# Logits of blocks 0 and 2 spread over other steps, and tile 7's normalisation and transposes moved

## The chip, the cores and the metric

The kernel runs on one core of a Trainium2 chip. The metric is the device time of one execution in microseconds (us), smaller is better. The core's engines run side by side, each through its own list of instructions in order, and wait for one another by semaphores: TensorE (PE, matmuls; PEld is its weight loading), VectorE (DVE), ScalarE (ACT), GpSimd (POOL) and SyncE (SP, which here only issues transfers). Matmuls write into banks of PSUM, and a bank can be written anew only when its readers are done.

## The reference

Three parts follow one another: attention over keys and values that are pooled by 8, a feed-forward network with the activation elu, and a second one that is routed, each token going to one of 8 experts by the largest gate logit. q, k and v are 8 x 8 x 576 x 64 in float32, so there are 4608 tokens of width 512; the first network's inner width is 2048, each expert's 1024.

```python
def _attn_ref(q, k, v) -> np.ndarray:
    ...
    scale = 1.0 / np.sqrt(D)
    k_p = k.reshape(B, H, Sp, pool, D).mean(axis=3)
    v_p = v.reshape(B, H, Sp, pool, D).mean(axis=3)
    scores = scale * np.matmul(q, k_p.transpose(0, 1, 3, 2))
    scores = scores - np.max(scores, axis=-1, keepdims=True)
    attn = np.exp(scores)
    attn = attn / (np.sum(attn, axis=-1, keepdims=True) + 1e-09)
    return np.matmul(attn, v_p).astype(np.float32)

def _moe_ref(x, w_in, w_out) -> np.ndarray:
    h = x @ w_in
    alpha = 1.0
    g = np.where(h > 0.0, h, alpha * (np.exp(np.minimum(h, 0.0)) - 1.0))
    return (g @ w_out).astype(np.float32)

def _moe2_ref(x, w_gate, w1, w2) -> np.ndarray:
    ...
    logits = x @ w_gate
    expert_idx = np.argmax(logits, axis=1)
    ...
    for e in range(E):
        ...
        h = np.maximum(xe @ w1[e], 0.0)
        ye = h @ w2[e]
        out[mask] = gate_w[mask, None] * ye
    return out.astype(np.float32)
```

## The kernel before

The 4608 tokens are 36 tiles of 128, and three tiles make a block, so there are 12 blocks. The stretch in question runs attention and the first network for the blocks, and the gate for each block after it. It is cut into 192 *steps*: a step multiplies one block by one sixteenth of the first network's inner width. Blocks 0 and 1 share steps 0 to 31 in alternating groups (20 to 27 belong to block 1, 28 to 31 to block 0); from step 32 on each block has 16 steps in a row: block 2 has 32 to 47, block 3 has 48 to 63, block 4 has 64 to 79.

In step n, PE computes *h*, 12 matmuls (`g1_mm`, L507), into one of two h banks in turn, then what else is due, and last *y* of step n-2, 9 matmuls (`g2`, L549), which add up in three banks, one for each tile, over the block's steps. ACT and DVE make the elu out of h: ACT runs three activations (`elu_a`, L517 to L519, the last writes th), DVE two instructions (`elu_b`, L524 and L525, called *g* below). The second frees the h bank for step n+2. Then ACT casts g to gh (L531) and DVE takes the rest gl (L532): y is computed as a sum of products of such high and low parts. Weights of the first network are split in the same manner in steps 0 to 27; DVE's part of this are *bits* (L226 to L232) and wol (L246).

Everything else is hung into steps by a table: `at(n, slot, function)` puts a piece of work into a slot of step n, and `step(n)` runs the slots in a fixed order. What matters is the later half of it: `act_mid` stands just behind g, then come y's matmuls, `pe_end`, then `evac` and `y_evac`, which copies y out of its banks when a block's sum is complete, then `dve_mid`, gh and gl, `act_end` and `end`. This order is the order on each engine; nothing reorders it later.

Attention of a tile t takes: scores on PE (`s_mm`, L411, into two banks), maxima on DVE (L418), exponentials on ACT (L427), the normalisation on DVE (`s_norm`, L431 to L433), transposes on PE (`t_mm`, L463, into two banks) with their copies on ACT (`t_copy`, L471), or for tiles from 9 on a turn on DVE (L447) with copies (`q_move`, L455), and the product with the values (`pv_mm`, L480), copied as xh and xl (L493, L494) for the first network. The scores, transposes, pv and the position counts of the gate take their banks from one ring of three.

The gate of a block, placed by `route_at(blk, n0, per)`, computes 24 logits (8 experts by 3 tiles), each one DVE instruction over 128 x 512 elements (`r_logit`, L600), from the token rows yr and a row of gate weights that SP has loaded. `per` lists how many stand in each step from n0 on: the first of a step in `dve_mid`, the others at `end`. In the step after the last of them comes the *top* (`r_top`: maximum, comparison, exponentials), one later the *weights* (`r_weight`, L641 to L653), which complete the token rows and let SP store them by three transfers (L647), and two further on the position count on PE (`r_count`, L663 and L664, one bank) with the *put* on DVE at `end` (`r_put`, L669 to L673) and three table writes on GpSimd. The token rows of a block are one buffer, yr, used by each block in turn; the rows of block 0 were parked and came back in three spare tiles (part).

Of the kernel before, what the change touches and what calls it, by code (L numbers as in the profile page):

```python
# [10 lines left out]
F32 = mybir.dt.float32  # L11
# [8 lines left out]
P = 128  # L20
B, H, S, D = 8, 8, 576, 64
# [5 lines left out]
TB = 3  # L27
# [3 lines left out]
NF = DFF // P  # L31
NE = 8
# [66 lines left out]
def fused_kernel(ctx: ExitStack, tc: tile.TileContext, q, k, v, w_in, w_out, w_gate, w1, w2, cst, out):  # L99
# [38 lines left out]
    mrpool = ctx.enter_context(tc.tile_pool(name="mrpool", bufs=1, side="right"))  # L138
# [357 lines left out]
    ys, yrows, lgs, pes = {}, {}, {}, {}  # L496
# [74 lines left out]
        yr = y_rows(blk, fetched.pop(x) if x is not None else None)  # L571
        yrows[blk] = [yr[:, j] for j in range(TB)]

    fetched = {}

    def y_park(blk, x, plus=None):
        yr = y_rows(blk, fetched.pop(plus) if plus is not None else None)
# [2 lines left out]
    def y_fetch(x, j):  # L580
        t = spool.tile([P, S], F32, tag="st", name=f"part{x}_{j}")
        nc.sync.dma_start(t[:, :DM], yparts[x][j * P:(j + 1) * P, :])
        fetched.setdefault(x, []).append(t[:, :DM])
        if x == 2:
            yrows.setdefault(0, []).append(t[:, :ROW])

    def y_join():
        for j in range(TB):
            nc.vector.tensor_add(yrows[0][j][:, :DM], yrows[0][j][:, :DM], ys[0][j])
# [5 lines left out]

    def r_logit(blk, e, j):
        if (e, j) == (0, 0):
            lgs[blk] = mrpool.tile([P, TB, NE], F32, tag="lg", name=f"lg{blk}")
        junk = mrpool.tile([P, DM], BF16, tag="junk", name=f"junk{blk}_{e}_{j}")
        nc.vector.scalar_tensor_tensor(  # L600
            junk, yrows[blk][j][:, :DM], 1.0, pes[blk, e], op0=ALU.mult, op1=ALU.mult, accum_out=lgs[blk][:, j, e:e + 1]
        )

    def r_logits(blk, e):
        for j in range(TB):
            r_logit(blk, e, j)
# [84 lines left out]
    LAG = 2  # L691
# [3 lines left out]
    def at(n, slot, fn, *args):  # L695
        events.setdefault((n, slot), []).append((fn, args))
# [3 lines left out]
    def score_at(t, n):  # L700
        at(n, "pe_end" if t == 7 else "pe_mid", s_mm, t)
        for hh in range(2):
            at(n, "dve_mid" if t == 7 else "dve_pre", s_max, t, hh)
        at(n, "act_end" if t in (6, 7) else "act_mid", s_exp, t, 0)
        n += t not in (7, 8)
        at(n, "act_end" if t in (7, 8) else "act_mid", s_exp, t, 1)
        at(n, "dve_mid" if t == 6 else "end", s_norm, t)

    def turn_at(t, n):
        at(n + 1, "end", q_turn, t)  # L710
# [3 lines left out]
    def trans_at(t, n):  # L714
        at(n, "pe_end" if t in OUT else "pe_mid", t_mm, t)
        for hh in range(2):
            at(n, "act_end" if t in OUT else "act_mid", t_copy, t, hh, nc.scalar.copy)
        out = OUT.get(t, ((n, "pe_end"), (n + 1, "pre")))
        at(*out[0], pv_mm, t)
        at(*out[1], pv_copy, t)  # L720
# [1 line left out]
    at(2 * NF - 2, "end", s_wide)  # L722
    first_of = {b: b * S // P for b in range(B)}
    SCORE = {6: (20, "pe_mid"), 7: (24, "pe_mid"), 8: (28, "pe_mid")}
    TRANS = {6: 23, 7: 26, 8: 30}
    OUT = {
        6: ((28, "pe_end"), (29, "pre")),
        7: ((29, "pe_end"), (30, "pre")),
# [2 lines left out]
    for t in range(2 * TB, NT):  # L731
        if t not in SCORE:
            blk, j = divmod(t, TB)
            SCORE[t] = (NF * (blk - 1) + 5 * j - 2 if blk > 3 else 2 * NF - 1 + 5 * j, "pe_mid")
            if t > T_TURN:
                at(SCORE[t][0], "pe_mid", pv_mm, t - 1)
                at(SCORE[t][0], "act_mid", pv_copy, t - 1)
            at(SCORE[t][0] - 6, "end", a_load, t)
        else:
            at(SCORE[t][0] - 6, "end", a_load, t)  # L740
        score_at(t, SCORE[t][0])
        if t >= T_TURN:
            turn_at(t, SCORE[t][0] + (t == T_TURN))
        else:
            trans_at(t, TRANS[t])
    at(NF * (NBLK - 1) - 2, "pe_mid", pv_mm, NT - 1)
# [42 lines left out]
    for x, (w, c) in enumerate(chunks):  # L789
        n = 2 + x  # L790
# [11 lines left out]
    for j in range(TB):  # L802
        at(4 * QF + 1 + j + (j == 2), "end", y_fetch, 0, j)
        at(6 * QF + 2 + j, "end", y_fetch, 1, j)
        at(7 * QF + 1 + j, "act_end", y_fetch, 2, j)

    def route_at(blk, n0, per):
        at(n0 - 3, "end", r_gate_load, blk, 0)
        at(n0 - 2, "end", r_gate_load, blk, 1)
        at(n0 - 1, "end", r_gate_load, blk, 2)  # L810
        n = 0
        for x in range(NE * TB):
            e, j = divmod(x, TB)
            at(n0 + n, ("dve_mid", "end", "end", "end")[x - sum(per[:n])], r_logit, blk, e, j)
            if j == TB - 1 and e + 3 < NE:
                at(n0 + n, "end", r_gate_load, blk, e + 3)
            if x + 1 == sum(per[:n + 1]):
                n += 1
        n += n0
        at(n, "dve_mid", r_top, blk)  # L820
        at(n + 1, "dve_mid", r_weight, blk)
        if blk < last - 1:
            at(n + 3, "pe_mid", r_count, blk)
            at(n + 3, "end", r_put, blk)

    route_at(1, 30, [2, 3, 3, 1, 1, 2, 3, 3, 3, 3])
    route_at(0, 41, [2] + [3] * 6 + [2, 2])
    route_at(2, 3 * NF + LAG + 1, [2, 2, 2, 2, 3, 3, 3, 3, 4])
    for blk in range(3, last):
        route_at(blk, NF * (blk + 1) + LAG, [3, 2, 3, 2, 3, 2, 3, 2, 2, 2])  # L830

# [663 lines left out]
    for k in range(1, len(main)):  # L1495
        kind, prev = main[k][0], main[k - 1][0]
        for u in range(TILES[kind]):
            if kind == "T":
                n = 4 * k - 2
            elif prev == "T":  # L1500
                n = 4 * k - TILES[kind] + u
            else:
                n = 4 * k - 1
            (trans_late if prev != "T" and u > 1 else trans_at).setdefault(n, []).append((main[k], u))
    moves, casts_first = {}, set()
    for k in range(TURN_FROM, len(main)):
        it, far = main[k], main[k - 1][0] == "T"
        if it[0] != "T":
# [3 lines left out]
            n = 4 * k - 4 if far else 4 * k - 1  # L1512
# [21 lines left out]
    def logits(n):  # L1534
        for x in range(6 * n, 6 * n + 6):
            e, j = divmod(x, TB)
            r_logit(last, e, j)
            if j == TB - 1 and e + 3 < NE:
                r_gate_load(last, e + 3)
# [166 lines left out]
```

## Time and profile before

| | |
|---|---|
| median of 3 runs | 1350.76 us (1349.97 to 1350.95) |
| the profiled execution | 1353.46 us, its span 1351.7 us |
| PE busy | 1333.7 us, 99% of the span |
| DVE busy | 1034.3 us, 77% |
| ACT busy | 813.0 us, 60% |
| GpSimd busy | 206.0 us, 15% |
| chain that ended last | PE 81%, DVE 7%, issue 5%, ACT 3%, DMA 3% |

The profile is of one execution. A row of a timeline gives the start and the length of an instruction (or of some alike in a row, "x4") and in brackets how long the engine had idled before it, and which instruction released it. Matmuls are pipelined, so that the lengths of neighbours overlap: distances from start to start are to be used. The chain that ended last is followed back from the last instruction, at each step to what released it.

### The profile page before, as it was taken

To read this page: it belongs to the slowest core of one execution; us is meant where nothing else is said; L and a number is where in the kernel's file an instruction comes from. 1 tells how busy PE (TensorE), PEld (TensorE's weight loads), DVE (VectorE), ACT (ScalarE), POOL (GpSimd) and SP (SyncE) were. 2 spreads that over 40 slices of the span, in tenths; PEclk is the share of its full clock that TensorE was granted. 3 is DMA by queue.
4 is the path that set the end of the run, shared out by engine and by line. 5 is a ranking of instruction groups with operands and counts; after the bars stand their busy time and mean duration, and the time that the engine had idled before them with its cause. 6 is when DMAs were issued, how large, how long until landed. Compare 5 with 4: busy or idle time off the path is not lost.

```text
span 1351.7 us, 23691 instructions
## 1 busy us (share of the span) xinstructions
PE 1333.7 (99%) x8365; PEld 1149.8 (85%) x8366; DVE 1034.3 (77%) x2463; ACT 813.0 (60%) x1977; POOL 206.0 (15%) x208
## 2 busy tenths in 40 slices
PE   8999999999999999999999999999999999999998
PEld 5799888888888889888888888988887888778787
DVE  7899888998887879797978787885768666646371
ACT  6777766676767676676666665562455444535261
POOL 0011011101111211111210000020313142112020
PEclk9999999999999999999999999999999999999999
DMA  9257443657464574545571432466577357758470
GB/s 344 76 175 211 124 100 82 87 77 71 72 86 74 69 85 56 93 65 81 70 98 48 64 36 52 79 167 122 180 132 157 124 180 265 261 198 309 148 272 24
DMA packets 109146, 169.43 MB, mean 125 GB/s; under 512 B 15510, under 2 KB 53016, under 8 KB 109017
## 3 DMA queue, kind: packets, MB, share of 16 engines
q1 hardware_dynamic: 91528, 135.45, 41.6%
q0 software_dynamic: 17488, 32.37, 13.0%
q8 instruction: 68, 1.11, 0.4%
q14 instruction: 62, 0.50, 0.2%
HBM read 146.35 MB, written 21.88 MB: 124 GB/s over the span
## 4 chain that ended last, share of the span: by engine, by line
PE 81%; DVE 7%; issue 5%; ACT 3%; DMA 3%; POOL 0%; SPq 0%; POOLq 0%; ACTq 0%; DVEq 0%
PE h L507 26%; PE y L549 25%; PE mhD L1297 12%; PE myD L1334 12%; PE pv L480 2%; DVE junk L600 2%; PE sp L411 1%; DMA w2stD<-in_moe_w_dram 1%; DVE g L524 1%; DMA wgb<-in_moe_w_gate_dram 1%; DVE g L525 1%; PE vsum L346 1%; ACT s L427 1%; DVE gl L532 1%; DMA natv<-in_v_dram 0%
## 5 line engine op out<-in xcount | busy, mean ns | idle before, releaser
L549 PE MATMUL y<-woh,gh 128*128 128x512 f32 x576 | 230.1, 399 | 0.6 <-DVE yr L567 0.3
L549 PE MATMUL y<-woh,gl 128*128 128x512 f32 x576 | 226.6, 393 | 0.0
L549 PE MATMUL y<-wol,gh 128*128 128x512 f32 x576 | 226.4, 393 | 0.0
L600 DVE SCALAR_TENSOR_TENSOR junk<-yr,wgb 128x512 bf16<-128x512 f32 x264 | 180.7, 685 | 6.7 <-DMA wgb<-in_moe_w_gate_dram 2.6
L531 ACT CAST gh<-g 128x384 fp32r<-128x384 f32 x192 | 98.6, 513 | 131.8 <-DVE g L525 111.6
L507 PE MATMUL h<-xh,wih 128*128 128x384 f32 x768 | 167.9, 340 | 2.6 <-ACT xh L493 1.5
L507 PE MATMUL h<-xl,wih 128*128 128x384 f32 x768 | 165.8, 337 | 0.0
L507 PE MATMUL h<-xh,wil 128*128 128x384 f32 x768 | 165.3, 336 | 0.0
L524 DVE SCALAR_TENSOR_TENSOR g<-g,th 128x384 f32<-128x384 f32 x192 | 106.3, 554 | 73.4 <-ACT th L519 72.5
L507 PEld LDWEIGHTS h<-xh,wih 128*128 128x128 f32 x768 | 138.4, 188 | 20.0 <-DVE g L525 2.6
L517 ACT ACTIVATE th<-h 128x384 f32<-128x384 f32 x192 | 94.2, 490 | 89.3 <-PE h L507 86.9
L1311 ACT ACTIVATE hhD<-mhD 128x512 fp32r<-128x512 f32 x64 | 38.2, 598 | 169.5 <-PE myD L1334 166.8
L507 PEld LDWEIGHTS h<-xl,wih 128*128 128x128 f32 x768 | 137.0, 188 | 0.2
L507 PEld LDWEIGHTS h<-xh,wil 128*128 128x128 f32 x768 | 137.0, 188 | 0.0
L1312 DVE SCALAR_TENSOR_TENSOR hlD<-mhD,hhD 128x512 fp32r<-128x512 f32 x64 | 44.0, 690 | 112.6 <-ACT hhD L1311 112.6
L549 PEld LDWEIGHTS y<-woh,gl 128*128 128x128 f32 x576 | 108.2, 188 | 23.6
L549 PEld LDWEIGHTS y<-woh,gh 128*128 128x128 f32 x576 | 108.1, 188 | 21.2 <-DVE yr L567 0.7
L549 PEld LDWEIGHTS y<-wol,gh 128*128 128x128 f32 x576 | 108.3, 188 | 16.7
L532 DVE TENSOR_TENSOR gl<-g,gh 128x384 fp32r<-128x384 f32 x192 | 106.8, 556 | 19.6 <-ACT gh L531 16.8
L525 DVE TENSOR_TENSOR g<-g,h 128x384 f32<-128x384 f32 x192 | 106.3, 554 | 6.6
L519 ACT ACTIVATE th<-th 128x384 f32<-128x384 f32 x192 | 100.9, 525 | 6.1
L518 ACT ACTIVATE g<-th 128x384 f32<-128x384 f32 x192 | 100.8, 525 | 6.1
(239 smaller groups left out, 2402.5 us busy)
## 6 DMA issues: line engine op xcount, KB each, us to landing
wgb<-in_moe_w_gate_dram SPq DMA_DIRECT2D x96, 256.0 KB
w1stD<-in_moe_w_dram SPq DMA_DIRECT2D x32, 512.0 KB
w2stD<-in_moe_w_dram SPq DMA_DIRECT2D x32, 512.0 KB
qT<-in_q_dram SPq DMA_DIRECT2D x36, 256.0 KB
ybuf<-yr SPq DMA_DIRECT2D x33, 256.5 KB
raw<-in_moe_w_in_dram SPq DMA_DIRECT2D x16, 512.0 KB
raw<-in_moe_w_out_dram SPq DMA_DIRECT2D x15, 512.0 KB
t1U<-in_moe_w_dram SPq DMA_DIRECT2D x12, 512.0 KB
```

The lines of the kernel that those rows point to most:

```text
L507: mark["g1"] = nc.tensor.matmul(ps, wi[i][a][:, c, o:o + P], bb[blk][:, c, :], start=n == 0, stop=n == 3 * KC - 1).ins
L517: nc.scalar.activation(th, hps[blk, f], AF.Relu, scale=-1.0)
L518: nc.scalar.activation(g, th, AF.Exp, scale=-1.0)
L519: nc.scalar.activation(th, th, AF.Tanh, scale=-0.5)
L524: nc.vector.scalar_tensor_tensor(g, g, 1.0, th, op0=ALU.add, op1=ALU.mult)
L525: nc.vector.tensor_max(g, g, hps.pop((blk, f)))
L531: nc.scalar.copy(gh, g)
L532: nc.vector.tensor_sub(gl, g, gh)
L549: nc.tensor.matmul(ys[blk][j], a[:, js], wo[i][bb][:, o, :], start=n == 0 and f in FIRST[blk], stop=n == 2 and f in LAST[blk],)
L600: nc.vector.scalar_tensor_tensor(junk, yrows[blk][j][:, :DM], 1.0, pes[blk, e], op0=ALU.mult, op1=ALU.mult, accum_out=lgs[blk][:, j, e:e + 1])
L1297: mark["g1"] = nc.tensor.matmul(ps[:, x], a[:, c, o * P:(o + 1) * P], y[:, c], start=k == 0, stop=k == len(terms) - 1).ins
L1334: nc.tensor.matmul(yps[it][u], a[:, us], second[w][:, o], start=i == 0 and o == 0 and n == 0, stop=i == 3 and o == 1 and n == 2,)
```

## The change

```diff
--- before.py
+++ after.py
@@ -571,7 +571,7 @@
         yr = y_rows(blk, fetched.pop(x) if x is not None else None)
         yrows[blk] = [yr[:, j] for j in range(TB)]
 
-    fetched = {}
+    fetched, spare = {}, {}
 
     def y_park(blk, x, plus=None):
         yr = y_rows(blk, fetched.pop(plus) if plus is not None else None)
@@ -583,6 +583,8 @@
         fetched.setdefault(x, []).append(t[:, :DM])
         if x == 2:
             yrows.setdefault(0, []).append(t[:, :ROW])
+            if j == 0:
+                spare["lg"] = t[:, S - TB * NE:]
 
     def y_join():
         for j in range(TB):
@@ -595,7 +597,10 @@
 
     def r_logit(blk, e, j):
         if (e, j) == (0, 0):
-            lgs[blk] = mrpool.tile([P, TB, NE], F32, tag="lg", name=f"lg{blk}")
+            if blk:
+                lgs[blk] = mrpool.tile([P, TB, NE], F32, tag="lg", name=f"lg{blk}")
+            else:
+                lgs[blk] = spare["lg"].rearrange("p (j e) -> p j e", j=TB)
         junk = mrpool.tile([P, DM], BF16, tag="junk", name=f"junk{blk}_{e}_{j}")
         nc.vector.scalar_tensor_tensor(
             junk, yrows[blk][j][:, :DM], 1.0, pes[blk, e], op0=ALU.mult, op1=ALU.mult, accum_out=lgs[blk][:, j, e:e + 1]
@@ -704,7 +709,10 @@
         at(n, "act_end" if t in (6, 7) else "act_mid", s_exp, t, 0)
         n += t not in (7, 8)
         at(n, "act_end" if t in (7, 8) else "act_mid", s_exp, t, 1)
-        at(n, "dve_mid" if t == 6 else "end", s_norm, t)
+        if t == 7:
+            at(n + 1, "act_mid", s_norm, t)
+        else:
+            at(n, "dve_mid" if t == 6 else "end", s_norm, t)
 
     def turn_at(t, n):
         at(n + 1, "end", q_turn, t)
@@ -722,7 +730,7 @@
     at(2 * NF - 2, "end", s_wide)
     first_of = {b: b * S // P for b in range(B)}
     SCORE = {6: (20, "pe_mid"), 7: (24, "pe_mid"), 8: (28, "pe_mid")}
-    TRANS = {6: 23, 7: 26, 8: 30}
+    TRANS = {6: 23, 7: 27, 8: 30}
     OUT = {
         6: ((28, "pe_end"), (29, "pre")),
         7: ((29, "pe_end"), (30, "pre")),
@@ -824,8 +832,8 @@
             at(n + 3, "end", r_put, blk)
 
     route_at(1, 30, [2, 3, 3, 1, 1, 2, 3, 3, 3, 3])
-    route_at(0, 41, [2] + [3] * 6 + [2, 2])
-    route_at(2, 3 * NF + LAG + 1, [2, 2, 2, 2, 3, 3, 3, 3, 4])
+    route_at(0, 40, [2] * 12)
+    route_at(2, 52, [2, 2, 3, 2, 3, 2, 3, 2, 3, 2])
     for blk in range(3, last):
         route_at(blk, NF * (blk + 1) + LAG, [3, 2, 3, 2, 3, 2, 3, 2, 2, 2])
```

Block 0's logits were in steps 41 to 49 (2, six times 3, 2, 2), its top in 50, weights in 51, count and put in 53. Now they are in steps 40 to 51, two in each, with the top in 52, the weights in 53, count and put in 55. Block 2's logits were in steps 51 to 59, top 60, weights 61, count and put 63; now they are in 52 to 61, top 62, weights 63, count and put 65. The loads of gate weights move along with them. Block 0's table of logits lies in the unused last 24 columns of the first of the three spare tiles, since it is still in use when block 2's begins. The normalisation of tile 7 moves from the end of step 24 to behind g of step 25, its transposes and their copies from step 26 to step 27. The number of instructions of each engine stays the same.

Where tile 7's copies stand on ACT: aTp7 are the two banks of transposes, aT7 what is copied out of them, gh1_14 and gh1_15 the casts of steps 26 and 27. Before:

```order
L531 CAST gh1_14_1988<-g1_14_1949 128x384
L471 COPY aT7_1992<-aTp7_0_1970 72x8x64
L471 COPY aT7_1992<-aTp7_1_1971 72x8x64
L517 ACTIVATE th1_15_2016<-h1_15_1997 128x384
L518 ACTIVATE g1_15_2015<-th1_15_2016 128x384
L519 ACTIVATE th1_15_2016<-th1_15_2016 128x384
L243 CAST woh7_1911<-dec15_1_1955 128x512
L531 CAST gh1_15_2033<-g1_15_2015 128x384
```

After, in the same place:

```order
L531 CAST gh1_14_1970<-g1_14_1949 128x384
L517 ACTIVATE th1_15_1995<-h1_15_1976 128x384
L518 ACTIVATE g1_15_1994<-th1_15_1995 128x384
L519 ACTIVATE th1_15_1995<-th1_15_1995 128x384
L243 CAST woh7_1908<-dec15_1_1955 128x512
L531 CAST gh1_15_2030<-g1_15_1994 128x384
L471 COPY aT7_2034<-aTp7_0_2012 72x8x64
L471 COPY aT7_2034<-aTp7_1_2013 72x8x64
```

The two copies, which stood behind the cast of step 26, stand behind that of step 27, whose g comes from DVE in that step.

Block 0's put on DVE: rpe0 to rpi0 are the put, pos0 is the bank of the position count, junk2_... are logits of block 2, mx14 are the maxima of tile 14, g3_6 and g3_7 belong to steps 54 and 55. Before:

```order
L600 SCALAR_TENSOR_TENSOR junk2_1_1_3545,lg2_3447<-yr2_3293,wgb2_1_3312 128x512
L532 TENSOR_TENSOR gl3_5_3548<-g3_5_3523,gh3_5_3547 128x384
L669 TENSOR_TENSOR rpe0_3444<-pos0_3520,small_70 128x24
L670 COPY acc_74<-acc_74 128x8
L671 TENSOR_TENSOR rpe0_3444<-rpe0_3444,roh0_3439 128x24
L672 TENSOR_REDUCE rpf0_3445<-rpe0_3444 128x3
L673 CAST rpi0_3446<-rpf0_3445 128x3
L600 SCALAR_TENSOR_TENSOR junk2_1_2_3559,lg2_3447<-yr2_3293,wgb2_1_3312 128x512
L524 SCALAR_TENSOR_TENSOR g3_6_3576<-g3_6_3576,th3_6_3577 128x384
L525 TENSOR_TENSOR g3_6_3576<-g3_6_3576,h3_6_3563 128x384
```

After:

```order
L524 SCALAR_TENSOR_TENSOR g3_7_3608<-g3_7_3608,th3_7_3609 128x384
L525 TENSOR_TENSOR g3_7_3608<-g3_7_3608,h3_7_3592 128x384
L605 SCALAR_TENSOR_TENSOR junk2_2_1_3624,lg2_3464<-yr2_3282,wgb2_2_3423 128x512
L532 TENSOR_TENSOR gl3_7_3627<-g3_7_3608,gh3_7_3626 128x384
L674 TENSOR_TENSOR rpe0_3532<-pos0_3605,small_70 128x24
L675 COPY acc_74<-acc_74 128x8
L676 TENSOR_TENSOR rpe0_3532<-rpe0_3532,roh0_3527 128x24
L677 TENSOR_REDUCE rpf0_3533<-rpe0_3532 128x3
L678 CAST rpi0_3534<-rpf0_3533 128x3
L605 SCALAR_TENSOR_TENSOR junk2_2_2_3638,lg2_3464<-yr2_3282,wgb2_2_3423 128x512
L418 TENSOR_REDUCE mx14_3672<-sp14_0_3674 128x4
L418 TENSOR_REDUCE mx14_3672<-sp14_1_3675 128x4
```

The put stood between g3_5 and g3_6, in step 53. Now it stands behind g3_7 and gl3_7, and the maxima of tile 14 follow it after one logit.

Block 2's weights on DVE: rse2 to acc are the weights, yr2 the token rows that they complete, gl3_13 and gl3_15 the rests of steps 61 and 63. Before:

```order
L524 SCALAR_TENSOR_TENSOR g3_13_3937<-g3_13_3937,th3_13_3938 128x384
L525 TENSOR_TENSOR g3_13_3937<-g3_13_3937,h3_13_3924 128x384
L641 TENSOR_REDUCE rse2_3953<-lg2_3447 128x3
L642 TENSOR_SCALAR rse2_3953<-rse2_3953 128x3
L644 RECIPROCAL yr2_3293<-rse2_3953 128x1 x3
L648 TENSOR_TENSOR req2_3915<-req2_3915,small_70 128x24
L649 TENSOR_REDUCE rmx2_3913<-req2_3915 128x3
L651 TENSOR_TENSOR roh2_3964<-req2_3915,rmx2_3913 128x24
L653 TENSOR_TENSOR acc_74<-acc_74,roh2_3964 128x8 x3
L532 TENSOR_TENSOR gl3_13_3973<-g3_13_3937,gh3_13_3972 128x384
L418 TENSOR_REDUCE mx15_4001<-sp15_0_4003 128x4
```

After:

```order
L524 SCALAR_TENSOR_TENSOR g3_15_4043<-g3_15_4043,th3_15_4044 128x384
L525 TENSOR_TENSOR g3_15_4043<-g3_15_4043,h3_15_4030 128x384
L646 TENSOR_REDUCE rse2_4063<-lg2_3464 128x3
L647 TENSOR_SCALAR rse2_4063<-rse2_4063 128x3
L649 RECIPROCAL yr2_3282<-rse2_4063 128x1 x3
L653 TENSOR_TENSOR req2_4021<-req2_4021,small_70 128x24
L654 TENSOR_REDUCE rmx2_4019<-req2_4021 128x3
L656 TENSOR_TENSOR roh2_4074<-req2_4021,rmx2_4019 128x24
L658 TENSOR_TENSOR acc_74<-acc_74,roh2_4074 128x8 x3
L532 TENSOR_TENSOR gl3_15_4083<-g3_15_4043,gh3_15_4082 128x384
L431 TENSOR_SCALAR sm15_3976<-sm15_3976 128x8
```

The weights moved from behind g3_13 to behind g3_15, two steps on. What writes the next block's token rows, in step 65, did not move.

## Rows read from the trace of the kernel before

**Rows 1.** the page, busy time of TensorE, share of the span, instructions
```profile
PE 1333.7 (99%) x8365; PEld 1149.8 (85%) x8366; DVE 1034.3 (77%) x2463; ACT 813.0 (60%) x1977; POOL 206.0 (15%) x208
```

**Rows 2.** timeline of TensorE: start us, us, engine, line, operation [idle before <-releaser]
```profile
160.61 0.96 PE L507 MATMUL h<-xh,wih 128*128 128x384 f32 x4 [0.48 <-DVE g L525]
...
167.07 0.73 PE L411 MATMUL sp<-kT,qT 64*64 64x72 f32 x32
...
245.87 0.86 PE L507 MATMUL h<-xh,wih 128*128 128x384 f32 x4
...
250.67 0.96 PE L507 MATMUL h<-xh,wih 128*128 128x384 f32 x4 [0.49 <-DVE g L525]
...
265.11 0.86 PE L507 MATMUL h<-xh,wih 128*128 128x384 f32 x4
...
273.95 0.50 PE L549 MATMUL y<-woh,gh 128*128 128x512 f32 x1 [0.28 <-DVE yr L567]
...
274.75 0.86 PE L507 MATMUL h<-xh,wih 128*128 128x384 f32 x4
...
293.38 0.86 PE L507 MATMUL h<-xh,wih 128*128 128x384 f32 x4
...
297.53 0.86 PE L507 MATMUL h<-xh,wih 128*128 128x384 f32 x4
...
300.79 0.73 PE L411 MATMUL sp<-kT,qT 64*64 64x72 f32 x32
...
320.23 0.86 PE L507 MATMUL h<-xh,wih 128*128 128x384 f32 x4
...
324.69 0.96 PE L507 MATMUL h<-xh,wih 128*128 128x384 f32 x4
```

**Rows 3.** timeline of VectorE, steps 25 to 27
```profile
156.50 0.17 DVE L431 TENSOR_SCALAR sm<-sm 128x8 f32<-128x8 f32 x1 [1.77 <-ACT s L427]
...
157.62 0.42 DVE L226 TENSOR_SCALAR dec<-dec 128x512 uint32<-128x512 uint32 x1
...
159.41 0.55 DVE L524 SCALAR_TENSOR_TENSOR g<-g,th 128x384 f32<-128x384 f32 x1
...
168.35 0.55 DVE L525 TENSOR_TENSOR g<-g,h 128x384 f32<-128x384 f32 x1
```

**Rows 4.** timeline of ScalarE, steps 25 and 26
```profile
157.44 0.53 ACT L519 ACTIVATE th<-th 128x384 f32<-128x384 f32 x1
...
165.16 1.06 ACT L471 COPY aT<-aTp 72x512 f32<-72x512 f32 x2
```

**Rows 5.** timeline of VectorE, steps 52 to 55
```profile
282.35 0.17 DVE L641 TENSOR_REDUCE rse<-lg 128x3 f32<-128x24 f32 x1
...
284.05 0.68 DVE L600 SCALAR_TENSOR_TENSOR junk<-yr,wgb 128x512 bf16<-128x512 f32 x1
...
291.99 0.88 DVE L455 COPY aT<-turned 32x256 f32<-32x256 f32 x3
...
293.97 0.17 DVE L669 TENSOR_TENSOR rpe<-pos,small 128x24 f32<-128x24 f32 x1
```

**Rows 6.** timelines of TensorE and VectorE, step 77
```profile
393.46 0.87 PE L507 MATMUL h<-xh,wih 128*128 128x384 f32 x4
...
397.47 0.56 DVE L524 SCALAR_TENSOR_TENSOR g<-g,th 128x384 f32<-128x384 f32 x1 [0.99 <-ACT th L519]
```

**Rows 7.** timeline of SyncE's queue, the row stores of step 77
```profile
399.20 1.47 SPq L647 DMA_DIRECT2D ybuf<-yr  x3
```

**Rows 8.** chain that ended last, 300 to 345 us: start us, us, what
```profile
305.81 11.00 DMA wgb<-in_moe_w_gate_dram
```

**Rows 9.** DMA issues: what, KB each, median us to landing
```profile
kT<-in_k_dram POOLq DMA_DIRECT2D x42, 144.0 KB, 3.4
```

**Rows 10.** windows: us, busy (x) by engine, PEclk, DMA share, GB/s
```profile
30.00:35.00 5.00, 5.00 (x22) 4.94 (x22) 4.60 (x10) 3.02 (x6) 0.85 (x2) 0.51 0.98 372
```

**Rows 11.** waits of TensorE: us in total, times, longest us
```profile
PE mhD L1297 <- DVE hlD L1312: 2.5, 2, 1.4
```

## The prediction

> **What bounds the kernel now.** I read the page's busy times first: TensorE (PE) is busy for 99% of the span [rows 1], so a change pays only through gaps between matmuls, and costs where it opens one. I then went through PE's own timeline from step to step, looking for steps longer than the usual pace. That pace is 4.15 us, the distance of the first h matmuls of steps 55 and 56, 293.38 and 297.53 [rows 2]. In the stretch that the change touches four places are longer (starts and waits of A, C, D and E all from [rows 2]). (A) The h of step 27 waits 0.48 for VectorE's (DVE's) g at 160.61. (C) Step 45 starts at 245.87 and step 46 at 250.67: 4.80, so 0.65 too long, with a wait of 0.49 for g. (D) Steps 49 and 50 take from 265.11 to 274.75, 9.64 for two paces of 8.30: 1.34 too long, part of it at 273.95 in a wait for DVE's yr copy. (E) Step 61 takes from 320.23 to 324.69, 4.46: 0.31. All four name DVE, or ScalarE (ACT) and DVE emptying banks, so DVE that runs late is what the change can cure. Then I followed DVE and ACT in the same stretches, and asked of every moved instruction who waits for it.
>
> **Tile 7: normalisation behind g(25), transposes from step 26 to 27.** Before, DVE idles 1.77 until the exponentials of tile 7 are done, runs the normalisation (156.50 to 157.62, 1.12), and only then bits(25) and g(25), at 159.41 [rows 3]. Behind g(25) the normalisation no longer holds g up: g(25) is bounded by ACT's third elu instruction, which ends at 157.44 + 0.53 = 157.97 [rows 4], 1.4 earlier. Gap A goes, and h(27) may start some 0.6 earlier. With that alone I would count a gain of 0.6.
>
> But the second half adds a wait. ACT's copy of tile 7's transposes out of their bank stood behind gh(26), at 165.16 [rows 4]. Now it stands behind gh(27), and gh(27) needs g(27) from DVE. The scores of tile 8, in step 28, start at 167.07 [rows 2] and their second bank is the one that this copy empties. When is it done? In the trace DVE goes from g(25) at 159.41 to the end of g(27) at 168.35 + 0.55 = 168.90 without a gap [rows 3]: 9.49 of work. Afterwards the same run has the normalisation in it as well: 157.97 + 9.49 + 1.12 = 168.6. gh(27) takes 0.5, and the first of the two copies half of 1.06 [rows 4], so the bank is free at 169.6. PE would have come to these scores at 167.07 - 0.6 = 166.5. It waits 3.1, and the scores come 169.6 - 167.1 = **2.5 us later than before**. Queued behind the waiting matmul on PE are y of step 26, pv of tile 6 and all later steps, and nothing overtakes. The bounds are 1.8 (the gh and copy pass at once, and DVE saves another 0.5) and 3.0. DVE and ACT are not held up by it: they get slack, but the time is lost for PE.
>
> **Block 0's and block 2's logits.** The number of instructions doesn't change. Block 0's 24 logits start a step earlier and go two to a step. Counted over the steps, after 46 to 49 three or four fewer of them have been issued than before, each about 0.65 [rows 5], so DVE is 2 to 2.6 us ahead where C and D stood: 0.65 and 1.34 go. The later start of block 2's takes three to five off steps 57 to 59, and E goes: 0.31, and about as much again in the two steps after it, 0.6 as an estimate. Together **-2.6**, between -1.3 (only half of it: DVE has its copies and turns there still) and -2.7. The additional two at step 40 fall into a step where DVE idles; I count nothing for them, at most 0.6 if they don't. Logits of block 0 in the spare columns of a parked tile cost nothing: same shape, same engine, and that tile isn't reloaded afterwards.
>
> Block 0's tail moves two steps, and this adds the second wait. The position count of block 0 now runs in step 55, and what reads its bank, the first instruction of the put on DVE, stands at the end of step 55. Step 56 computes the scores of tile 14, whose second bank is that bank (the ring has three; in between lie pv 13 and the first score bank). Before, the count ran in step 53. DVE at that time: g(52) starts 4.01 after its step's start where nothing holds it, as 393.46 to 397.47 shows for step 77 [rows 6]. Step 52 starts at 280.79 - 2.0 = 278.7 after the gains, so at 282.7. Before, the run from block 0's weights at 282.35 to its put at 293.97 takes 11.62 [rows 5] and holds the weights, 5 logits, 3 gl, 2 g pairs, a normalisation, a turn, and 3 of 6 turned copies. The new run from g(52) to the put holds all this and 3 more logits (3 x 0.65), a gl (0.5), two more g pairs (2 x 1.1), the other copies (0.9) and block 0's top (some 0.6): 6.15. So it reaches the put at 282.7 + 11.62 + 6.15 = 300.5, and the bank is free at 300.6. PE would be at these scores at 300.79 [rows 2] - 2.0 = 298.8. **+1.8**, with bounds 0.8 and 2.8 for one or two logits of error. Behind it on PE again is everything; on DVE the maxima of tile 14.
>
> **Block 2's tail** moves from step 61 to 63 (weights) and this adds the third. The weights are written into the token rows yr, and SyncE (SP) then stores these rows by three 256.5 KB transfers. The copies that take the next block's y out of PE's banks, behind step 65, write the same buffer: they wait until all three transfers have landed. Before, four steps lay between; now two. From the start of a weight step to the first issue it is 399.20 - 393.46 = 5.74 [rows 6, 7]. The trace shows no landing for these transfers. The nearest row of the same queue and size is a gate load of 256 KB that took 11.00 from issue to landing and stood on the chain [rows 8]; far off it is the 3.4 of a 144 KB transfer on GpSimd's queue [rows 9]. I take the 11.00: same queue, and three go out together, over 1.47 [rows 7]; I count it from half a us after the first issue. The rows are free at start + 5.74 + 0.5 + 11.0 = 17.2, the first copy ends 0.6 later at 17.8. PE needs that bank for y in step 66, that is 3 paces, half a step for h, and some 0.2 for the position count: 3 x 4.15 + 2.1 + 0.2 = 14.7 after the start of step 63. **+3.1**; by the 3.4 it would be 0, and with a DVE late by a logit or two 4.5. Behind the waiting copies stand gh(65) on ACT and gl(65) on DVE; both have two paces until they are needed, so they add nothing.
>
> **Sum.** 2.5 - 2.6 + 1.8 + 3.1 = +4.8. The profiled execution took 1353.46, its span 1351.7 and 1.76 around it, 2.7 above the median of the runs. I add the sum to the median: 1350.76 + 4.8 = **1355.6 us**.
>
> **Rivals.**
> *Faster (5%).* The three waits have cover that I don't see, and only the relief counts: -0.6 for A and -2.6, 1347.6 us. For it speaks that the DVE chain does run through C, D and E. It decides at three points: the copy behind gh(27) done by 166.5, the put's first instruction by 298.8, the rows' landing by 14 after step 63's start. Against it: the first is bounded by ACT's 157.97 and 9.49 of DVE work that can't shrink.
> *Same (17%).* One of the later waits doesn't bite, most likely that of the rows, since a landing of under 8 us would free them in time: 4.8 - 3.1 = +1.7, 1352.5 us; without the put's wait too it is -0.1. For it: its duration is the one that I haven't seen. Against it: three transfers together, beside others, are hardly quicker than one.
> *Slower by the clock (8%).* [...]
> *No relief (5%).* The waits come, but DVE's lateness only moves to other steps: +7.4 with A still gone, 1358.2 us.
>
> **Chances and range.** The forecast has 65%. Faster by over 0.2% (2.7 us, about what a measurement of this kernel can tell from no change): 5%. Within: 17%. Slower: 78%. The range takes the lower ends of the three waits that are likely (1.8, 0.8, 1.5) with the full relief, +1.5, and at the top the two slow rivals: 1352.2 to 1358.2.
>
> **What would show it.** Right: PE waits of 2 to 3.5 us for ACT's aT copy near 166.5, of 1 to 3 for DVE's rpe near 301, of 2 to 4 for ACT's yr near 348; no g or yr wait left at C, D and E; the clock at 1.00 in these stretches. Wrong: one of the three is missing, or the waits of C and D turn up at steps 51 to 55, where g(54) has only half a us to spare in my count.

## The result, and the profile after

| | median | lowest to highest | runs |
|---|---|---|---|
| before | 1350.37 us | 1349.24 to 1351.43 | 6 |
| after | 1358.71 us | 1357.07 to 1363.8 | 6 |

The ratio is 1.0067, 95% interval 1.0056 to 1.0079. The change made the kernel 8.3 us slower; 1355.6 was forecast, and 1358.71 lies half a us above the range. The profiled execution of the changed kernel took 1362.44 us, its span is 1360.6, against 1351.7 before: 8.9 more. So this profile shows somewhat more than the median's loss.

PE works 5 us more than before [rows 1], though it does the same matmuls. From the page (busy us, share of the span, instructions):

```profile
PE 1338.7 (98%) x8366; PEld 1154.6 (85%) x8366; DVE 1034.3 (76%) x2463; ACT 813.2 (60%) x1977; POOL 205.6 (15%) x208
```

The waits of TensorE in the whole span (us in total, times, longest) are led by the three new ones. Of these groups the kernel before had only y for ACT yr, with 0.2:

```profile
PE sp L411 <- ACT aT L471: 2.5, 1, 2.5
PE y L549 <- ACT yr L565: 2.5, 1, 2.5
PE sp L411 <- DVE rpe L674: 1.7, 1, 1.7
```

**Step 28, the scores of tile 8.** TensorE's timeline after, from the step's first h matmul to the next step's (start us, us, engine, line, operation, idle before it and its releaser; some rows left out):

```profile
164.58 0.97 PE L507 MATMUL h<-xh,wih 128*128 128x384 f32 x4
...
169.78 0.72 PE L411 MATMUL sp<-kT,qT 64*64 64x72 f32 x30 [2.55 <-ACT aT L471]
...
171.40 0.63 PE L549 MATMUL y<-woh,gl 128*128 128x512 f32 x1
...
173.95 0.39 PE L549 MATMUL y<-woh,gl 128*128 128x512 f32 x1
...
175.30 0.96 PE L507 MATMUL h<-xh,wih 128*128 128x384 f32 x4
```

The step takes 10.72 us, 164.58 to 175.30; before it took 6.16 (h at 164.86 and 171.02). The scores wait 2.55 for aT. But look at the y matmuls behind the wait: most take 0.63, until 173.95, where one has 0.39 again. In step 28 of the kernel before they have some 0.39, and the granted clock there (the third number from the right in the window below) is 1.00:

```profile
168.30 0.39 PE L549 MATMUL y<-woh,gl 128*128 128x512 f32 x1
```

```profile
155.00:172.00 17.00, 16.52 (x134) 14.11 (x133) 14.64 (x30) 13.59 (x40) 0.00 (x0) 1.00 0.30 97
```

VectorE in steps 25 to 27 (g of step 25, the normalisation, the end of g of step 27) and ScalarE's cast and copies:

```profile
158.34 0.56 DVE L524 SCALAR_TENSOR_TENSOR g<-g,th 128x384 f32<-128x384 f32 x1 [1.47 <-ACT th L519]
...
160.01 0.17 DVE L431 TENSOR_SCALAR sm<-sm 128x8 f32<-128x8 f32 x1
...
168.09 0.55 DVE L525 TENSOR_TENSOR g<-g,h 128x384 f32<-128x384 f32 x1
```

```profile
168.73 0.51 ACT L531 CAST gh<-g 128x384 fp32r<-128x384 f32 x1 [0.49 <-DVE g L525]
169.15 1.06 ACT L471 COPY aT<-aTp 72x512 f32<-72x512 f32 x2
```

g of step 25 starts when th is there, the normalisation runs behind it, g of step 27 ends at 168.09 + 0.55 = 168.64, the copies start at 169.15, and the scores go on at 169.78. In [rows 3, 4] the copies stood at 165.16 and nothing waited for them.

**Step 56, the scores of tile 14.** TensorE, and the first instruction of block 0's put on VectorE:

```profile
300.38 0.86 PE L507 MATMUL h<-xh,wih 128*128 128x384 f32 x4
...
305.66 0.72 PE L411 MATMUL sp<-kT,qT 64*64 64x72 f32 x30 [1.68 <-DVE rpe L674]
...
308.01 0.63 PE L549 MATMUL y<-woh,gl 128*128 128x512 f32 x1
...
314.21 0.86 PE L507 MATMUL h<-xh,wih 128*128 128x384 f32 x4
```

```profile
305.43 0.18 DVE L674 TENSOR_TENSOR rpe<-pos,small 128x24 f32<-128x24 f32 x1
```

The put's first instruction runs at 305.43 and the scores go on at 305.66, after 1.68 of idle. Again most of the y matmuls behind it take 0.63. Steps 56 and 57 take 314.21 - 300.38 = 13.83, against 6.11 + 4.15 = 10.26 before: 3.57 more.

**Step 66, y of block 4.** TensorE; the chain of work that ended last (start, us, what):

```profile
349.44 0.86 PE L507 MATMUL h<-xh,wih 128*128 128x384 f32 x4
...
354.20 0.50 PE L549 MATMUL y<-woh,gh 128*128 128x512 f32 x1 [2.52 <-ACT yr L565]
...
355.54 0.63 PE L549 MATMUL y<-wol,gh 128*128 128x512 f32 x1
...
364.01 0.87 PE L507 MATMUL h<-xh,wih 128*128 128x384 f32 x4
```

```profile
344.00 9.46 DMA ybuf<-yr
```

The copies wait for the row stores, whose last one stands on the chain with 9.46, up to 353.46; ScalarE's copy follows at 353.56. Steps 66 and 67 take 14.57, against 10.21 before (343.68 to 353.89): 4.36 more, of which 2.52 are the wait.

What the three have in common is in the windows (columns: stretch; its length and the busy us of PE, PEld, DVE, ACT, POOL with their instructions; then PE's granted clock, DMA share, GB/s), the first wait and the 4 us behind each of the three:

```profile
165.00:169.70 4.70, 2.23 (x14) 1.83 (x12) 4.50 (x11) 3.22 (x8) 0.00 (x0) 1.00 0.36 102
170.50:174.50 4.00, 4.00 (x14) 2.95 (x15) 1.94 (x4) 2.70 (x12) 0.00 (x0) 0.57 0.59 153
...
306.30:310.30 4.00, 4.00 (x17) 3.23 (x12) 3.73 (x10) 2.43 (x11) 1.21 (x1) 0.59 0.40 120
...
354.20:358.20 4.00, 4.00 (x11) 3.26 (x12) 2.48 (x11) 3.59 (x8) 0.86 (x1) 0.58 0.34 81
```

During the first wait the granted clock still reads 1.00. Behind each wait it is 0.57 to 0.59 over 4 us: most of that stretch ran at half clock (0.50 from 171.0 to 173.5, from 309.0 to 310.0 and from 355.0 to 358.0). A clock that runs at 0.57 for 4 us gives 1.7 us less work, and that is about what the three places have lost beyond the price of the waits (last column of the table below).

**The relief** came as forecast. Steps 45, 50, 61 and 63 are 0.64, 1.13, 0.31 and 0.36 shorter (0.14 of the last is the position count's move to step 65), and step 26, with its wait for g [rows 2], is 1.28 shorter, of which 0.64 is the transposes' move to step 27. None of A, C, D and E has a wait left.

| | forecast | in the two profiles | of it clock |
|---|---|---|---|
| steps 26 to 28 | +2.5 | +3.9 | 1.8 |
| steps 45 to 50, 61 to 63 | -2.6 | -2.7 | |
| steps 56 and 57 | +1.8 | +3.6 | 1.6 |
| steps 66 and 67 | +3.1 | +4.4 | 1.6 |

The last column is the length of the three places less what they take at full clock: 8.97 for step 28 (run e10), 2.0 more than before at 56 (e1, e5, e10), 2.75 more at 66 (e1). Without it the middle column makes 4.2, with it 9.2; the spans differ by 8.9, since the rest of the kernel gives 0.3 back.

### The profile page after: what moved, and what is told of

Its sections match the earlier page's. It is cut to its first block, busy times and chain, and to the rows that moved or that the text cites. A ratio compares the mean times of both kernels' runs of the same rounds, so it can differ in the third digit from the quotient of the medians.

```text
span 1360.6 us, 23692 instructions
## 1 busy us (share of the span) xinstructions
PE 1338.7 (98%) x8366; PEld 1154.6 (85%) x8366; DVE 1034.3 (76%) x2463; ACT 813.2 (60%) x1977; POOL 205.6 (15%) x208
## 4 chain that ended last, share of the span: by engine, by line
PE 87%; issue 4%; DVE 3%; DMA 3%; ACT 2%; POOL 0%; SPq 0%; POOLq 0%; ACTq 0%; DVEq 0%
PE y L549 29%; PE h L507 29%; PE mhD L1305 12%; PE myD L1342 12%; PE pv L480 3%; PE sp L411 2%; DMA w2stD<-in_moe_w_dram 1%; DMA ybuf<-yr 1%; PE vsum L346 1%; DMA natv<-in_v_dram 0%; PE ksum L359 0%; PE uh L1386 0%; DMA kst<-in_k_dram 0%; DVE zmD L1203 0%; DVE junk L605 0%
```

## The experiments

The theory: each new wait costs its own time, and TensorE, having idled, then runs some 3.5 us at half clock (170.43 to 173.95 in step 28). The rivals: the time beyond the waits comes from engines that were held up; or it belongs to that one execution. The kernel before ran beside each group of runs and took 1351.15, 1351.4 and 1351.3 us there (24, 21 and 21 runs, 1348.5 to 1358.1); differences below are from the ratios, times 1351.

**Tile 7 as before, the logits as after (e1_t7).**

```diff
-        if t == 7:
-            at(n + 1, "act_mid", s_norm, t)
-        else:
-            at(n, "dve_mid" if t == 6 else "end", s_norm, t)
+        at(n, "dve_mid" if t == 6 else "end", s_norm, t)
...
-    TRANS = {6: 23, 7: 27, 8: 30}
+    TRANS = {6: 23, 7: 26, 8: 30}
```

Expected: 

> Tile 7's part of the change undone (normalisation at the end of step 24, transposes and copies in step 26), the logits as in the changed kernel. Theory (each new wait costs its idle time and then some 3.5 us at half clock): steps 26 to 29 fall back to the lengths of before, so the +3.9 us found there go and the 0.5 wait for g at step 27 returns: about 1354.8 us, granted clock 1.00 there, while the half-clock stretches behind steps 56 and 66 stay. Rival (the wait alone counts, and what is lost beyond it has another cause): only 2.4 go, about 1356.3, and a half-clock stretch stays near 170.

Measured: 1356.77 us, 5.0 over before (3.4 to 6.8), 9 runs from 1353.55 to 1358.26. The time alone doesn't tell 4.4 from 5.9. The profile does: steps 26 to 29 have the lengths of before and no slow y. It also showed something that I hadn't expected. The waits at 56 and 66 are there, 1.67 and 2.50, but no half clock follows. TensorE at step 56, and the window behind it:

```profile
300.80 0.72 PE L411 MATMUL sp<-kT,qT 64*64 64x72 f32 x30 [1.67 <-DVE rpe L674]
...
302.26 0.39 PE L549 MATMUL y<-woh,gh 128*128 128x512 f32 x1
```

```profile
301.50:305.50 4.00, 4.00 (x23) 3.61 (x21) 3.97 (x11) 2.37 (x11) 1.22 (x1) 1.00 0.53 140
```

After the same idle as in the changed kernel, 1.67 against 1.68, y has 0.39 and the clock 1.00; step 56 is 2.0 longer than before, step 66 2.75. So the waits' own price is seen clean here, and half clock doesn't follow every idle of this length.

**Block 0's put ahead of g (e2_put).**

```diff
-            at(n + 3, "end", r_put, blk)
+            at(n + 3, "dve_pre" if blk == 0 else "end", r_put, blk)
```

Expected: 

> The changed kernel, but block 0's put runs on DVE ahead of g of step 55 instead of behind gl of step 55; everything else as it is. Theory: the bank of the position count is read some 2 us earlier, the scores of tile 14 no longer wait (under 0.3), the clock stays at 1.00 after step 56, and the 3.5 us of steps 56 and 57 go: about 1355.2 us. Rival (DVE is late there whatever the order, and the put in front only holds up g of step 55 and then h of step 57): 1357 to 1358.7 with a wait for DVE g at step 57.

Measured: 1357.71 us, 5.9 over before (3.6 to 8.2), 4 runs. The longest wait of TensorE between 140 and 400 us:

```profile
PE y L549 <- ACT yr L565: 3.8, 1, 3.8
```

The wait for rpe is gone and step 56 is back at its length of before, with no wait for g at 57; so the place of the put was the cause. The gain in time is less than the 3.5 expected, though four runs don't tell the two apart. In the profile the rows landed later: 3.8 of wait at step 66 instead of 2.5, with half clock behind it and behind the wait of step 28. The stores stand where they stood, and e5 below, which doesn't touch the order at all, has 3.6 there: the landing varies without a change of the order.

**Block 2's weights a step earlier (e3_w62).**

```diff
-    route_at(2, 52, [2, 2, 3, 2, 3, 2, 3, 2, 3, 2])
+    route_at(2, 52, [2, 2, 3, 2, 3, 3, 3, 3, 3])
```

Expected: 

> The changed kernel, but block 2's logits go over nine steps (2, 2, 3, 2, 3, 3, 3, 3, 3 from step 52), so that its weights stand in step 62 instead of 63 and its put in 64. Theory: the rows land before the copies of step 65 need them (18.5 us after the start of step 62 against 20.8), the wait of step 66 and the half clock behind it go, 4.4 us: about 1354.3, or up to 0.6 more if the denser logits make DVE late at steps 60 to 62. Rival (the landing is set by what else is in flight, not by its issue): the copies wait as long as now and the time stays at 1358.7.

Measured: 1356.29 us, 3.6 over before (1.6 to 5.7), 10 runs from 1352.51 to 1359.3. The rival's 8.3 is out. Waits of TensorE between 140 and 560 us:

```profile
PE sp L411 <- ACT aT L471: 2.5, 1, 2.5
PE h L507 <- DVE g L525: 2.2, 1, 2.2
PE sp L411 <- DVE rpe L674: 1.8, 1, 1.8
```

The wait for yr is gone. Step 28 has its half clock, step 56 with 1.82 of idle has not. The 2.2 for g is new: in step 104, far from the change, a gate load landed late and held DVE up (5.80 of idle); no half clock followed (1.00 over the 4 us behind). Such a wait is in some of the profiles below as well.

**The first two waits filled with matmuls (e5_fill).** 20 and 12 more matmuls of 128 x 288 into the scores' first bank, ahead of the scores; these overwrite it.

```diff
+    FILL = {8: (0, 12, 20), 14: (3, 8, 12)}
...
+        if t in FILL:
+            blk, f, count = FILL[t]
+            for _ in range(count):
+                nc.tensor.matmul(
+                    ps[0].rearrange("p a s -> p (a s)"),
+                    wi[f // 2][0][:, 0, (f % 2) * P:(f % 2 + 1) * P],
+                    xh[blk][:, 0, :4 * SP],
+                    start=True,
+                    stop=True,
+                )
```

Expected: 

> The changed kernel with 20 more matmuls ahead of the scores of tile 8 and 12 ahead of those of tile 14, into a bank that the scores overwrite, so that PE works while it would have waited; what the scores wait for is untouched. Theory (the loss beyond the idle time is the clock, which falls because PE idles): the scores start when they did, the clock stays at 1.00 behind them, and 1.5 us at each of the two places go: about 1355.7 us. Rival (the loss beyond the idle time comes from engines that were held up): nothing goes, 1358.7 or slightly more, with y of steps 28 and 56 as slow as now.

Measured: 1357.48 us, 6.1 over before (4.3 to 7.8), 10 runs. The one wait left between 140 and 400 us (lines are shifted by 12 here):

```profile
PE y L561 <- ACT yr L577: 3.6, 1, 3.6
```

Step 28 takes 9.15 instead of 10.72, step 56 8.11 instead of 9.34 with its y at 0.39: though the scores come hardly earlier (the bulk of them 4.96 us behind the step's first h in step 28, where it was 5.20), what came behind them is as fast as ever. That leaves no room at these two places for engines that were held up. Step 66, not filled, waited 3.6 and had its half clock.

**One wait alone, in the kernel before (e8_wait).**

```diff
-            at(n, "act_end" if t in OUT else "act_mid", t_copy, t, hh, nc.scalar.copy)
+            at(n + (t == 7), "act_end" if t in OUT else "act_mid", t_copy, t, hh, nc.scalar.copy)
```

Expected: 

> The kernel before with a single new wait: tile 7's two copies moved behind gh of step 27, everything else as before (transposes in step 26, normalisation ahead of g). Theory: the scores of tile 8 come 3.0 later (copies at 169.4 to 170.0 instead of 165.2), and half clock behind it costs 1.5: 4.5 over the kernel before; in executions in which the clock holds only 3.0. Rival (DVE's and ACT's slack behind the wait gives part of it back at steps 45 to 63): 1 to 2 over the kernel before.

Measured: 1355.19 us, 4.05 over before (2.6 to 5.5), 8 runs from 1351.25 to 1358.39; the rival's 1 to 2 is out. The profiled execution took 1351.25. TensorE at step 28:

```profile
167.36 0.72 PE L411 MATMUL sp<-kT,qT 64*64 64x72 f32 x30 [2.36 <-ACT aT L471]
...
168.59 0.39 PE L549 MATMUL y<-woh,gl 128*128 128x512 f32 x1
```

2.36 of idle, and y at 0.39 behind it, so no half clock: step 28 is 2.70 longer than before. The median is 1.3 above that price. That would fit half clock in most of the other executions: their mean granted clock was 0.996 each, that of the profiled one 0.998. It is a hint only, as the kernel before has 0.995 to 0.998 from execution to execution.

**Tile 7's transposes and copies earlier in step 27 (e6_copy7).**

```diff
-        at(n, "pe_end" if t in OUT else "pe_mid", t_mm, t)
+        at(n, "pe_end" if t in (6, 8) else "pe_mid", t_mm, t)
...
-            at(n, "act_end" if t in OUT else "act_mid", t_copy, t, hh, nc.scalar.copy)
+            at(n, "dve_pre" if t == 7 else "act_end" if t in OUT else "act_mid", t_copy, t, hh, nc.scalar.copy)
```

Expected: 

> The changed kernel, but tile 7's transposes at the middle of step 27 and their copies on ACT ahead of that step's elu; normalisation behind g of step 25 as in the changed kernel, the logits too. Theory (what costs at step 28 is the copies' place behind gh of step 27, not the later normalisation): the wait for aT goes and the 0.6 of step 27 stays gained, so 4.5 us under the changed kernel, 3 to 4 over the kernel before, and a little under the run with tile 7's part undone. Rival (the normalisation behind g is itself too late for the transposes): a wait of 0.5 to 1.5 for the transposes or the scores stays in steps 27 and 28.

Measured: 1358.77 us, 6.75 over before (4.5 to 9.1), but 4 runs only, so not the 3 to 4 expected. Waits of TensorE between 140 and 400 us:

```profile
PE y L549 <- ACT yr L565: 2.7, 1, 2.7
PE sp L411 <- DVE rpe L674: 1.8, 1, 1.8
```

The wait for aT is gone and the gain of step 26 stays, so the copies' place was the cause, not the later normalisation. Both other waits had half clock behind them in this profile: steps 56 and 66 are 3.6 and 4.5 longer than before, and steps 26 to 67 together 5.4. This was the fastest of the four executions, with a mean clock of 0.995; the others had 0.992 to 0.993. The expectation had left the clock out.

**All three waits taken away (e4_all)**: the edits of e2, e3 and e6 together.

Expected: 

> The changed kernel with all three new waits taken away and its reliefs kept: tile 7's transposes at the middle of step 27 and their copies on ACT ahead of that step's elu (normalisation still behind g of step 25), block 0's put ahead of g of step 55, block 2's logits over nine steps with the weights in step 62. Theory (relief 2.6 at steps 45, 49, 50 and 61 to 63, relief 0.6 at step 27, nothing else): 3.2 us under the kernel before, no PE wait over 0.4 in steps 20 to 70 and the clock at 1.00 there. Rival (the reliefs come only because the waits give DVE time to catch up): no faster than before, with waits for DVE g at steps 46 to 62.

Measured: 1349.69 us, 1.35 under before, interval from 3.1 under to 0.4 over, so not told from no change. The longest wait of TensorE between 140 and 400 us:

```profile
PE y L549 <- ACT yr L565: 0.4, 1, 0.4
```

Steps 26, 45, 50 and 63 are as short as in the changed kernel, none of the three waits is left as it was, and no y is slow. But step 61 is as long as before (4.51), and y of step 66 still waits 0.45 for the rows.

**All three waits filled (e7_fill3, e10_fill3b), with the changed kernel as control (e11_after).** e7 adds to e5 20 matmuls into a free bank ahead of y of step 66. e10 also turns the ring back, so that later banks are those of the changed kernel:

```diff
+    def fill_y():
+        busy(bank([P, 4 * SP], "fill66"), 4, 2, 20)
+        turns["a"] = (turns["a"] - 1) % 3
+
+    at(66, "pe_mid", fill_y)
```

`busy` is the loop of e5. Expected of e7: 

> The changed kernel with PE kept at work in all three waits: 20 more matmuls ahead of the scores of tile 8, 12 ahead of those of tile 14, 20 ahead of y of step 66, all into banks that are free and not read. Theory (the waits alone are worth 2.35 + 2.0 + 2.75 less 2.6 of relief, and the rest is the clock): 4.5 us over the kernel before, clock at 1.00 behind all three places, so 3.8 under the changed kernel's 8.3. Rival (the extra matmuls only move the loss, or the clock has nothing to do with idle time): 7 to 9 over the kernel before, with half-clock stretches behind the three places.

Measured: 1359.25 us, 7.6 over before (5.0 to 10.1), 8 runs: a miss of the 4.5. Its profile has the clock at 1.00 behind all three places, but a late gate load with a wait of 0.9 at step 104. Was the filling worthless, or the bank ring the reason? Expected of the control: 

> The changed kernel once more, unchanged, as the control for the run with filled waits. Theory (the three waits last about as long each time, and the clock falls behind an idle of 1.7 to 3 us in some executions and in others not): waits of 2.5, 1.7 and 2.5 to 3.8 again, half clock behind one to three of them, 7 to 8.5 over the kernel before. Rival (the half clock belongs to that one execution): no half clock behind the waits, 4.5 over the kernel before.

Expected of e10: 

> The changed kernel with PE kept at work in all three waits, as in the earlier run with three fills, but with the order of the banks behind step 66 kept as it is in the changed kernel. Theory: clock at 1.00 behind all three places; 4.5 to 5.5 over the kernel before and 2 to 4 under the control. Rival (filling the waits buys nothing, as the median of the earlier run suggests): as slow as the control.

Measured side by side on one chip: the control 1363.19 us, 10.0 over before (7.3 to 12.7; 6 runs from 1359.84 to 1366.57); e10 1357.64 us, 6.1 over (4.2 to 8.1; 10 runs from 1356.27 to 1362.46). 5.5 us lie between the medians, 3.9 between the two differences, though e10 does more matmuls. The control's profiled execution was the slowest of its six, that of e10 the second fastest of its ten. TensorE of e10 in step 28 (lines shifted by 14), with the filling where the idle was, and the windows behind the three places:

```profile
162.20 0.96 PE L521 MATMUL h<-xh,wih 128*128 128x384 f32 x4
...
164.39 2.83 PE L401 MATMUL sp<-xh,wih 128*128 128x288 f32 x20
167.15 0.81 PE L425 MATMUL sp<-kT,qT 64*64 64x72 f32 x32
...
168.44 0.40 PE L563 MATMUL y<-woh,gl 128*128 128x512 f32 x1
...
171.17 0.97 PE L521 MATMUL h<-xh,wih 128*128 128x384 f32 x4
```

```profile
167.90:171.90 4.00, 4.00 (x32) 3.17 (x30) 2.49 (x5) 3.88 (x19) 0.00 (x0) 1.00 0.64 164
...
302.30:306.30 4.00, 4.00 (x23) 3.62 (x21) 3.97 (x11) 2.37 (x11) 1.22 (x1) 1.00 0.40 142
...
349.30:353.30 4.00, 4.00 (x20) 3.63 (x21) 2.47 (x11) 3.55 (x8) 0.85 (x1) 1.00 0.59 151
```

The step takes 8.97 from h to h, y has 0.39 or 0.40, and the clock is 1.00 behind all three. The control's waits, between 140 and 560 us, are those of the first profile again, and one for a late gate load:

```profile
PE y L549 <- ACT yr L565: 2.5, 1, 2.5
PE sp L411 <- ACT aT L471: 2.4, 1, 2.4
PE h L507 <- DVE g L525: 2.1, 1, 2.1
PE sp L411 <- DVE rpe L674: 1.7, 1, 1.7
```

All four of the control's waits had half clock behind them. From step 26 to step 67 the control takes 9.7 more than the kernel before, e10 5.6 and e7 5.4. So the filling worked in e7 as it did in e10; outside these steps its profile has the 1.4 of step 104 on top, and that the ring had a part in its median is not shown. e10's 5.6 is more than the price of the waits at full clock since its rows landed late: behind the filling y still waits 0.54 for them, and step 66 takes 0.7 more than in e1.

**A version that beats both (e9_best)**: e4 with block 2's weights ahead of g of step 62.

```diff
-        at(n + 1, "dve_mid", r_weight, blk)
+        at(n + 1, "dve_pre" if blk == 2 else "dve_mid", r_weight, blk)
```

Expected: 

> All three waits taken away as in the earlier run, and block 2's weights ahead of g of step 62, so that its rows are stored some 1.5 us earlier and the 0.45 us wait of step 66 goes. Theory: no PE wait over 0.3 in steps 23 to 70 beside tile 6's, 3 us under the kernel before (1 to 4, since the run with the 0.45 us wait was 1.4 under). Rival (its gain is given back elsewhere): no faster than before.

Measured: 1348.83 us, ratio 0.9978 (0.9965 to 0.9992), 3.0 under before, 12 runs from 1346.84. Its profile has steps 26 to 67 only 1.8 shorter than before, so part of the 3.0 isn't located. The only wait of TensorE between 140 and 400 us:

```profile
PE y L549 <- ACT gh L531: 0.2, 1, 0.2
```

The profiled execution took 1356.43, and shows where an execution can still lose time: TensorE and VectorE at step 104,

```profile
520.26 1.46 PE L507 MATMUL h<-xh,wih 128*128 128x384 f32 x4 [2.74 <-DVE g L525]
```

```profile
518.44 0.69 DVE L605 SCALAR_TENSOR_TENSOR junk<-yr,wgb 128x512 bf16<-128x512 f32 x1 [6.34 <-DMA wgb<-in_moe_w_gate_dram]
```

where a gate load landed late, DVE idled 6.34 and PE 2.74. The h matmuls behind it take 1.46 for four instead of 0.87: half clock once more (granted clock 0.57 over 4 us), outside the change.

**Counted together**, the profiles hold 16 waits of 1.67 to 3.81 at steps 28, 56 and 66: 12 had half clock behind them, 4 (two in e1, one each in e3 and e8) had not, with idles of 1.67, 1.82, 2.36 and 2.50, lengths at which others fell. Of the 8 places that were filled none had it. Of three more waits, of 2.06 to 2.74 at step 104 (e11, e3, e9), two had it.

**The executions that were not profiled.** The mean granted clock of every execution is known as well, to 0.001. On average it was 0.9970 in the 66 runs of the kernel before that stood beside these, 0.9942 in the changed kernel's six and 0.9933 in the control's six, but 0.9969 in e10's ten. A clock that is lower by 0.0028 over 1360 us takes away 3.8 us of TensorE's work, one that is lower by 0.0037 5.0. The changed kernel lost 8.3 and the control 10.0, of which waits and relief explain some 4.2. So the half clock is no matter of the one profiled execution, and it has about the size of what is missing.

## Why the prediction was wrong

- *What bounds the kernel, and the relief*: right. Gaps A, C, D and E were DVE's, they closed, and -2.6 was -2.7 in the profiles.
- *Tile 7*: right in mechanism and nearly in time. The copies were forecast to free the bank at 169.6, and the scores went on at 169.78. At full clock the net price is 2.2 (step 28 of e10, 2.8, less 0.6 in steps 26 and 27) against 2.5.
- *Block 0's put*: right; at full clock 2.0 against 1.8.
- *Block 2's rows*: right; 2.75 against 3.1. The landing that I had no row for was 9.46 where the nearest row said 11.00. e2 had 1.3 more of wait, and its last store landed in 10.53.
- *The sum*: +4.8 forecast. With the prices at full clock it is 2.2 - 2.7 + 2.0 + 2.75 = +4.25.
- *The step that failed is the rival of the clock*, given 8%: the forecast has the clock at 1.00 and so puts its cost at nothing. Each of the three waits could bring half clock, and in 12 of 16 cases it came, at 1.6 to 1.8 us each in the changed kernel. 12 of 16 for three waits are 2.25 falls, at 1.6 each 3.6, and on 4.25 that makes 7.9, an estimate; measured are 8.3 (the interval is 7.6 to 10.7). The clock of before does hold behind its longest idle, 1.4 [rows 11], with 1.00 over the 4 us behind it; that did not show that it would hold behind 1.7 or 2.5. And the fall in [rows 10] itself spoke against going by the longest idle: it came at 30.1 us (the granted clock is 1.00 from 29.5 to 30.0, 0.58 from 30.0 to 30.5, 0.50 behind that), in the middle of 40 narrow matmuls, and in the 25 us ahead of it TensorE's longest idle is the one in the first of these rows of the kernel before:

```profile
25.19 0.97 PE L507 MATMUL h<-xh,wih 128*128 128x384 f32 x4 [0.69 <-ACT xh L493]
...
27.41 6.21 PE L359 MATMUL ksum<-sums,natk 128*128 128x16 f32 x40
```

The rival was also mis-sized: its 8% within the 78%, and its place at the top of the range, stand for a single fall at 5.00 x 0.49 = 2.4, from the 5 us of [rows 10]. No run shows a fall behind a wait at that price: in the changed kernel one cost 1.6 to 1.8, and there were three. At 1.6 each, one to three falls make 1350.76 + 4.8 + 1.6 to 4.8, 1357.2 to 1360.4, and with what the runs show that case would have carried most of the chance.

Left open: what decides whether half clock follows an idle of 1.7 to 2.5; why e10's 6.1 lies 1.9 above the 4.25 (0.7 of it are the late rows of its profile, and its interval begins at 4.2); and why a gate load at step 104 lands late in some executions.

## What to carry to other kernels

Moving a step to relieve one engine moves everything that reads its banks and buffers: look for the next user of each bank in the ring and each single buffer, and work out which one comes first now. A wait that a saturated TensorE did not have before should be priced at its length and, at lengths like these (1.7 to 3.8 us), at the half clock behind it as well: that cost 1.6 to 1.8 us at each place of the changed kernel, and it came behind 12 of the 16 waits here. To separate the two, fill the wait with matmuls whose result nobody reads.

## What the runs showed of the hardware

- The granted clock fell behind single idles of TensorE of 1.67 to 3.81 us in the middle of dense work; most y matmuls behind took 0.63 instead of 0.39, and the granted clock was 0.57 to 0.59 over the 4 us behind each wait of the changed kernel, most of that stretch at 0.50. Behind idles of the same length in other runs it stayed at 1.00 (1.67 and 2.50 in e1, 1.82 in e3, 2.36 in e8).
- The clock fell without a long idle too: at 30.1 us of the kernel before, with no idle over 0.69 in the 25 us ahead, it went to 0.50 until 36.9.
- Matmuls that nobody reads, put into such waits, left no half clock in 8 of 8 places (1.00 over the 4 us behind all three of e10), and with all three filled the kernel was 5.5 us faster at the median than the control beside it.
- The last of the same three row stores landed in 9.46 us (the changed kernel) and 10.53 (e2), and the wait for them was 2.45 to 3.81 in kernels with the same steps between issue and use.
